# A planned kernel of linear attention and two MLPs: left rows of the attention's units as operations of their own, product half first, 10 warm-up transpositions for 24, look-ahead 22 for 20

## The chip, the cores and the metric

One core of one Trainium2 chip runs the whole program. The metric is the device time in microseconds; lower is better. The engines are TensorE (PE; its weight loads are shown as PEld), VectorE (DVE), ScalarE (ACT), GpSimd (POOL) and SyncE (SP), which issues nearly all of the DMA transfers here.

## The reference

Inputs and result are float32, except the weights of the MLPs, which are float64 and reach the kernel as pairs of 32-bit words. The attention is linear: for 4 batches and 8 heads, with 576 rows of width 64, it forms `kv = k^T v` per head, then `out = q kv`, and divides each row by its root mean square. Two MLPs follow on the 2304 x 512 result.

```
kv  = einsum('bhsd,bhse->bhde', k, v)
out = einsum('bhsd,bhde->bhse', q, kv)
out = out / sqrt(mean(out*out, -1) + 1e-6) * g_norm
x   = out as (2304, 512)
x   = softplus(x @ w_in)   @ w_out      # 512 -> 2048 -> 512
x   = max(0.01*h, h) @ w_out2,  h = x @ w_in2
```

## The kernel before

**Units.** The attention works in 16 units of one batch and two heads (`T`, `O`, `X`; unit u belongs to batch u // 4). Of the 576 rows of a unit, 512 are loaded as four blocks of 128 (`lda`, five buffers for each of q, k and v), and the other 64, the left rows, are loaded once per batch for all heads (`ldr`, two buffers). `T(u)` copies q and k into `qp` and `kp`, transposes q on PE in two halves (`f_t`: j = 0 writes the first PSUM bank of the unit, with two blocks and the left rows; j = 1 writes the second, with two blocks), multiplies k by v (`f_kv`, L436 and L439, in the second bank), masks the product into `kvm` (L455, L458) and copies the two banks to `qt` (L384, L386). The operations on one PSUM bank follow each other, so the second half of `qt` is copied only when `kvm` has been made. `O(u)` multiplies `qt` by `kvm` (`f_o`, L473; left rows `f_l`, L479) and takes squares and sums. `normal(w)` takes the units 2w and 2w + 1 together: logarithm and exponential on ACT, three Newton steps (L523 to L525) and the scaled outputs `xn` and `xnl` (L535) on DVE. Two PSUM banks hold the outputs, so `O(2w + 2)` waits for the `xn` of unit 2w. `X(u)` transposes `xn` back (L557, L569) and scales it into `xy` (L545, L547), which the MLPs read.

**Around it.** The weights are decoded from float64 on ACT and DVE (`decode_pair`, L609 to L649) and split into two parts (`split_pair`, L667 to L700). The first two pairs of chunks are decoded while the attention starts. The MLPs (lines 842, 932, 1099 and 1104 are their matmuls) run behind it, as far as possible already between the last units. Ahead of everything PE transposes the identity `N_WARM` times (`warm`, L1205).

**The order.** A planner, `Plan`, writes the order of every queue. Each operation is given its engines with a cost, what it reads and what it writes. Its due time is the sum of PE costs ahead of it in the program; an operation off PE is given `AHEAD` more (14 for the two first pairs of weights). Going backwards, the due time is then drawn forward to that of each reader less a latency of 0.2 and its own span (for a DMA 0.57 + 1.1 + its cost + 1.0). `run` simulates the engines with these costs, takes for each the operation with the earliest due time among those ready within 0.4 us, and emits it. An engine works through its queue strictly in the emitted order. A PE operation is one entry of the plan: all of its matmuls wait for all that it reads.

Of the kernel before, what the change touches and what calls it, by code (L numbers as in the profile page):

```python
# [21 lines left out]
class Plan:  # L22
# [2 lines left out]


    LAT = 0.2
    AHEAD = 20.0
    SPARE = 2.0
    WAIT = 0.4  # L30
    IDLE = 40.0
# [9 lines left out]
    def op(self, cost, fn, reads=(), writes=(), due=None):  # L41
        o = {"cost": cost, "fn": fn, "succ": [], "n": len(self.ops)}
        deps = {}
        for k in reads:
            if k in self.writer:
                deps[self.writer[k]["n"]] = self.writer[k]
        for k in writes:
            for d in [self.writer.get(k), *self.readers.get(k, ())]:
                if d is not None:
                    deps[d["n"]] = d  # L50
        for k in reads:
            self.readers.setdefault(k, []).append(o)
        for k in writes:
            self.writer[k], self.readers[k] = o, []
        o["deps"] = list(deps.values())
        for d in o["deps"]:
            d["succ"].append(o)
        o["due"] = self.pe
        if "PE" in cost:
            self.pe += cost["PE"]  # L60
        else:
            o["due"] += self.AHEAD
        if due is not None:
            o["due"] = due
        self.ops.append(o)
        return o
# [67 lines left out]
def linear_attention_two_mlps(  # L134
# [32 lines left out]
    nc = tc.nc  # L167
# [3 lines left out]
    P = 128  # L171
# [23 lines left out]
    GF = 4  # L195
    NG = NF // GF
    XL = 4
    N_WARM = 24
    U_H = 10


# [2 lines left out]
    def ring(pool, name, n, shape, dt=F32):  # L204
        return [pool.tile(shape, dt, name=f"{name}{i}") for i in range(n)]

    ident = const.tile([P, P], F32, name="ident")
# [112 lines left out]
    ps = ring(psum, "ps", 8, [P, 512])  # L320
# [6 lines left out]
    NLD = 5  # L327
    lda = {nm: ring(attp, nm + "a", NLD, [P, 2, 4, D]) for nm in "qkv"}
    ldr = {nm: ring(attp, nm + "r", 2, [P, H, D]) for nm in "qkv"}
    qp = ring(attp, "qp", 2, [P, 4, 2, D])  # L330
    kp = ring(attp, "kp", 2, [P, 4, 2, D])
# [5 lines left out]
    xnl = ring(mstp, "xnl", 2, [P, 4, D])  # L337
# [12 lines left out]
    op = plan.op  # L350
# [11 lines left out]
    def xyk(kcs, c0, n):  # L362
        return [("xy", kc, c) for kc in kcs for c in range(c0 // 64, (c0 + n - 1) // 64 + 1)]

    def copy_to(out, in_, n, reads, writes, engines="ADP"):


        def fn(e):
            if e == "A":
                nc.scalar.activation(out, in_, AF.Copy)  # L370
            elif e == "D":
                nc.vector.tensor_copy(out, in_)
            else:
                nc.gpsimd.tensor_scalar(out, in_, 1.0, 0.0, ALU.mult, ALU.add)

        cost = {"A": t_a(n), "D": t_d(n, True), "P": 0.1 + n * 1.2e-3}
        op({e: cost[e] for e in engines}, fn, reads, writes)

    def from_psum(out, in_, n, bank, writes):


        def fn(e):
            if e == "A":
                nc.scalar.activation(out, in_, AF.Copy)  # L384
            else:
                nc.vector.tensor_copy(out, in_)  # L386

        return op({"A": t_a(n), "D": t_d(n)}, fn, [], [("ps", bank), *writes])
# [22 lines left out]
    def T(u):  # L411
        b, hp = u // NPAIR, u % NPAIR
        h2 = slice(2 * hp, 2 * hp + 2)
        i = u % 2
        for nm, dst in (("q", qp), ("k", kp)):
            copy_to(
                dst[i], lda[nm][u % NLD].rearrange("p h r d -> p r h d"), 512,
                [(nm, u % NLD)], [(nm + "p", i)], "AD" if u == 0 else "ADP",
            )
        p0 = 2 * i if u < U_H else 0  # L420
        p1 = p0 + 1
        kv = ps[p1][:, 2 * P:3 * P]
        ql, kl, vl = (ldr[nm][b % 2] for nm in "qkv")
        va = lda["v"][u % NLD]

        def f_t(e, j):
            for r in range(2):
                nc.tensor.transpose(  # L428
                    ps[p0 + j][:, r * P:(r + 1) * P], qp[i][:, 2 * j + r, :, :], ident
                )  # L430
            if j == 0:
                nc.tensor.transpose(ps[p0][:, 2 * P:3 * P], ql[:, h2, :], ident)

        def f_kv(e):
            for r in range(4):
                nc.tensor.matmul(  # L436
                    kv, kp[i][:, r, :, :], va[:, :, r, :], start=(r == 0), stop=False
                )
            nc.tensor.matmul(kv, kl[:, h2, :], vl[:, h2, :], start=False, stop=True)  # L439

        for j in range(2):
            n = (2 * P + RL, 2 * P)[j]
            c0 = (0, 2 * P + RL)[j]
            op(
                {"PE": 0.25}, lambda e, j=j: f_t(e, j),
                [("qp", i)] + ([] if j else [("qr", b % 2)]), [("ps", p0 + j)],
            )
            if j:
                op(
                    {"PE": 1.1}, f_kv,  # L450
                    [("kp", i), ("v", u % NLD), ("kr", b % 2), ("vr", b % 2)], [("ps", p1)],
                )
                def f_m(e):
                    if e == "D":
                        nc.vector.tensor_tensor(kvm[i], kv, mask, ALU.mult)  # L455
                        return
                    for h in (slice(0, D), slice(D, P)):
                        nc.scalar.activation(  # L458
                            kvm[i][:, h], kv[:, h], AF.Copy, scale=mask[:, h.start:h.start + 1]
                        )  # L460

                op({"D": 0.22, "A": 0.42}, f_m, [], [("ps", p1), ("kvm", i)])
            from_psum(qt[i][:, c0:c0 + n], ps[p0 + j][:, :n], n, p0 + j, [("qt", i, j)])
# [3 lines left out]
    def O(u):  # L467
        i = u % 2
        at_ = (0, P, 2 * P + RL, 3 * P + RL)

        def f_o(e):
            for r in range(4):
                nc.tensor.matmul(  # L473
                    ps[4 + i][:, r * P:(r + 1) * P], qt[i][:, at_[r]:at_[r] + P], kvm[i],
                    start=True, stop=True,
                )

        def f_l(e):
            nc.tensor.matmul(  # L479
                ps[6][:, i * P:(i + 1) * P], qt[i][:, 2 * P:3 * P], kvm[i],  # L480
                start=True, stop=True,
            )

        need = [("kvm", i), ("qt", i, 0), ("qt", i, 1)]
        op({"PE": 0.87}, f_o, need, [("ps", 4 + i)])
        op({"PE": 0.22}, f_l, need, [("ps", 6)])
        squares(ps[4 + i], ("ps", 4 + i), sq[i], ss[u // 2 % 2][:, 8 * i:8 * i + 8], ("sq", i),
                ("ss", u // 2 % 2, i), P, 8)

    def squares(o, ok, s_, sum_, sk, mk, p, n):  # L490
        op(
            {"A": t_a(n * D)},
            lambda e: nc.scalar.activation(s_, o.rearrange("p (g d) -> p g d", d=D), AF.Square),
            [], [ok, sk],
        )
        op(
            {"D": t_d(n * D)},
            lambda e: nc.vector.tensor_reduce(sum_, s_, axis=AX, op=ALU.add), [sk], [mk],  # L498
        )
# [51 lines left out]
    def X(u):  # L551
        b, hp = u // NPAIR, u % NPAIR
        i = u % 2

        def f_x(e):
            for r in range(4):
                nc.tensor.transpose(  # L557
                    ps[7][:, r * P:(r + 1) * P], xn[u % 4][:, 2 * r:2 * r + 2, :], ident
                )

        cm, cl = (b * S + RL, b * S) if b % 2 else (b * S, b * S + 4 * P)
        op({"PE": 0.44}, f_x, [("xn", u % 4)], [("ps", 7)])
        scaled(xy[:, hp, cm:cm + 4 * P], ps[7], 4 * P, 7, xyk([hp], cm, 4 * P))
        if i == 0:
            return

        def f_l(e):
            for t in range(2):
                nc.tensor.transpose(  # L569
                    ps[6][:, (2 + t) * P:(3 + t) * P], xnl[u // 2 % 2][:, 2 * t:2 * t + 2, :], ident,  # L570
                )

        op({"PE": 0.11}, f_l, [("xnl", u // 2 % 2)], [("ps", 6)])
        scaled(
            xy[:, hp - 1:hp + 1, cl:cl + RL],
            ps[6][:, 2 * P:4 * P].rearrange("p (a n) -> p a n", a=2)[:, :, :RL],
            2 * RL, 6, xyk([hp - 1, hp], cl, RL),
        )
# [75 lines left out]
    def decode_pair(F, which, i):  # L654

        for m in range(2):
            decode_w(F + m, which, half[i][m])
# [545 lines left out]
    def warm(e):  # L1203
        for _ in range(N_WARM):
            nc.tensor.transpose(ps[7][:, 0:P], ident, ident)  # L1205

    op({"PE": 0.0}, warm, (), [("ps", 7)], due=-100.0)
    for i in range(NU + XL):
        if i in (1, 2):
            plan.AHEAD = 14.0  # L1210
            decode_pair(2 * (i - 1), 0, 0)
            split_pair(0, i - 1, True)
            plan.AHEAD = Plan.AHEAD
        if i < NU:
# [26 lines left out]
    for s in range(2 * NT2 + 2):  # L1241
        t, u = s // 2, s % 2
# [98 lines left out]
```

## Time and profile before

| | us |
|---|---|
| median of 3 runs (785.46 to 786.5) | 785.85 |
| the profiled execution | 782.83 |
| its span, first to last instruction | 780.9 |
| PE busy in it | 769.2 (98%) |
| DVE busy in it | 683.7 (88%) |
| ACT busy in it | 544.9 (70%) |

A row of the timeline gives the start, the length, the engine, the line and the operation with its tiles, the count, and in brackets the engine's idle time ahead of it and what ended it. In a list of waits each row gives the total, the number of waits and the longest one. A row of the windows gives, for each engine, busy time and instructions in a stretch; PEclk is TensorE's granted clock as a share of full speed.

### The profile page before, as it was taken

How to read it: one execution, taken by the hardware profiler on the slowest of the kernel's cores; microseconds unless marked ns; L12 is line 12 of the kernel's file. 1: busy time of each engine (PE TensorE's matmuls, PEld its weight loads, DVE VectorE, ACT ScalarE, POOL GpSimd, SP SyncE). 2: the span in 40 equal slices, each digit the busy share in tenths (PEclk: the TensorE clock that was granted, in tenths of full speed). 3: DMA queues.
4: the chain of work that ended last, by engine and by line, in shares of the span. 5: the costliest groups of instructions: out<-in, count | busy, mean ns of one | idle time of the engine just before them, and what ended most of it. 6: DMA issues, size and time to landing. Idle time of an engine off the chain costs nothing.

```text
span 780.9 us, 13269 instructions
## 1 busy us (share of the span) xinstructions
PE 769.2 (98%) x5053; PEld 765.3 (98%) x5053; DVE 683.7 (88%) x1088; ACT 544.9 (70%) x923; POOL 21.0 (3%) x36
## 2 busy tenths in 40 slices
PE   7899999999999999999999999999999999999997
PEld 7899999999999999999999999999999999999997
DVE  6999999999899987996899999998899877886667
ACT  5889989888687755774589788885668645554441
POOL 3330000000000000000000000000000000000000
PEclk9999999999999999999999999999999999999999
DMA  9992758675885783773678969785875762563814
GB/s 313 324 332 84 305 203 314 260 290 182 347 296 184 287 329 103 283 285 111 247 285 299 328 226 417 308 303 181 325 259 180 289 253 102 212 232 108 309 42 121
DMA packets 80351, 192.48 MB, mean 246 GB/s; under 512 B 11552, under 2 KB 54560, under 8 KB 80288
## 3 DMA queue, kind: packets, MB, share of 16 engines
q1 hardware_dynamic: 78672, 190.86, 67.5%
q10 hardware_dynamic: 1616, 0.79, 0.3%
q8 instruction: 39, 0.64, 0.3%
q14 instruction: 24, 0.20, 0.1%
HBM read 152.31 MB, written 39.32 MB: 245 GB/s over the span
## 4 chain that ended last, share of the span: by engine, by line
PE 94%; DVE 2%; ACT 1%; SPq 1%; DMA 1%; issue 0%; ACTq 0%; DVEq 0%
PE ps L842 43%; PE ps L1099 23%; PE ps L1104 22%; PE ps L473 2%; PE ps L932 2%; PE ps L436 1%; DMA mf<-in_moe_w_in_dram 1%; PE ps L557 1%; PE ps L428 0%; DVE ra L688 0%; DVE ss L498 0%; SPq L396 0%; DVE xn L535 0%; PE ps L479 0%; DVE mf L667 0%
## 5 line engine op out<-in xcount | busy, mean ns | idle before, releaser
L842 PE MATMUL ps<-ra 128*128 128x384 f32 x1932 | 385.5, 335 | 0.0
L842 PEld LDWEIGHTS ps<-ra 128*128 128x128 f32 x1932 | 332.1, 188 | 0.0
L1099 PE MATMUL ps<-rb 128*128 128x256 f32 x1512 | 203.9, 282 | 0.0
L1104 PE MATMUL ps<-rb 128*128 128x384 f32 x1008 | 200.9, 334 | 0.0
L1099 PEld LDWEIGHTS ps<-rb 128*128 128x128 f32 x1512 | 198.0, 189 | 0.1
L871 ACT ACTIVATE rb<-mf 128x768 fp32r<-128x768 f32 x154 | 130.0, 846 | 69.0 <-PE ps L1099 38.0
L1104 PEld LDWEIGHTS ps<-rb 128*128 128x128 f32 x1008 | 177.0, 188 | 0.0
L876 DVE TENSOR_TENSOR rb<-mf,rb 128x768 fp32r<-128x768 f32 x154 | 146.5, 953 | 23.7 <-ACT rb L871 22.8
L722 DVE TENSOR_TENSOR xy<-ps,xy 128x384 f32<-128x384 f32 (+2 forms) x247 | 134.6, 549 | 33.8 <-PE ps L1099 22.3
L956 DVE TENSOR_TENSOR mf<-mf 128x768 f32<-128x768 f32 x68 | 64.1, 951 | 2.7 <-ACT mf L857 2.1
L1149 ACT ACTIVATE mf<-ps 128x384 f32<-128x384 f32 x92 | 44.6, 488 | 28.5 <-PE ps L842 26.7
L1156 DVE TENSOR_TENSOR mf<-ps,mf 128x384 f32<-128x384 f32 x92 | 50.7, 553 | 11.1 <-PE ps L842 9.6
L1161 ACT ACTIVATE ps<-ps 128x384 f32<-128x384 f32 x46 | 22.0, 479 | 24.2 <-PE ps L842 24.1
L857 ACT ACTIVATE mf<-mf 128x768 f32<-128x768 f32 x26 | 21.9, 843 | 17.9 <-DVE mf L1156 17.6
L1021 DVE TENSOR_TENSOR rb<-rc,rb 128x512 fp32r<-128x512 f32 x44 | 29.9, 683 | 0.7 <-ACT rb L1018 0.7
L1018 ACT ACTIVATE rb<-rc 128x512 fp32r<-128x512 f32 x44 | 27.5, 625 | 1.4 <-PE ps L1099 0.8
L863 ACT ACTIVATE mf<-mf 128x768 f32<-128x768 f32 x24 | 20.1, 839 | 9.3 <-DVE mf L1156 9.3
L1115 ACT ACTIVATE ps<-ps 128x384 f32<-128x384 f32 (+2 forms) x44 | 21.0, 479 | 6.9 <-PE ps L1104 3.9
L635 ACT ACTIVATE sqr<-mf 128x512 uint16<-128x512 uint16 x30 | 23.4, 781 | 0.0
L863 ACT ACTIVATE mf<-ps 128x384 f32<-128x384 f32 x32 | 15.7, 490 | 9.8 <-PE ps L842 9.6
L717 ACT ACTIVATE xy<-ps 128x384 f32<-128x384 f32 (+2 forms) x38 | 18.6, 494 | 3.8 <-PE ps L1099 1.7
L857 ACT ACTIVATE mf<-ps 128x384 f32<-128x384 f32 x32 | 15.4, 482 | 6.6 <-PE ps L842 6.4
(123 smaller groups left out, 757.8 us busy)
## 6 DMA issues: line engine op xcount, KB each, us to landing
ra<-xscr SPq DMA_DIRECT2D x131, 768.0 KB, 6.6
xscr<-ra SPq DMA_DIRECT2D x30, 768.0 KB, 4.4
mf<-in_moe_w_in_dram SPq DMA_DIRECT2D x18, 512.0 KB, 5.2
mf<-in_moe_w_out_dram SPq DMA_DIRECT2D x18, 512.0 KB, 6.3
lf<-in_moe_w_in_dram SPq DMA_DIRECT2D x14, 512.0 KB, 5.4
lf<-in_moe_w_out_dram SPq DMA_DIRECT2D x14, 512.0 KB, 5.6
xscr<-xy SPq DMA_DIRECT2D x8, 768.0 KB, 5.5
qa<-in_q_dram SPq DMA_DIRECT2D x16, 256.0 KB, 5.3
```

The lines of the kernel that those rows point to most:

```text
L722: {"D": t_d(n)}, lambda e: nc.vector.tensor_tensor(dst, src, dst, ALU.add),
L842: nc.tensor.matmul(o, w_[:, a, c:c + P], e_[:, b, kk, :], start=(not on and which < 2 and kk == 0 and n == 0), stop=(kk == 1 and n == 2), ...
L857: {"A": t_a(n)}, lambda e: nc.scalar.activation(dst(), src(), AF.Softplus),
L863: lambda e: nc.scalar.activation(dst(), src(), AF.Prelu, alpha=0.01),
L871: {"A": t_a(n)}, lambda e: nc.scalar.activation(g[:, 0, :, :], c.ap, AF.Copy),
L876: lambda e: nc.vector.tensor_tensor(g[:, 1, :, :], c.ap, g[:, 0, :, :].bitcast(F32), ALU.subtract),
L956: lambda e: nc.vector.tensor_tensor(to.ap, x.ap, y.ap, ALU.subtract),
L1021: lambda e: nc.vector.tensor_tensor(w_[:, 1], src(), w_[:, 0].bitcast(F32), ALU.subtract), sk + hk, lk,
L1099: nc.tensor.matmul(y[:, 256 * (j % 2):256 * (j % 2 + 1)], G_[:, a, m, js], w_[:, b, m, :], **flags)
L1104: nc.tensor.matmul(y[:, :BN], w_[:, a, m, js], G_[:, b, m, :], **flags)
L1149: {"A": t_a(BN)}, lambda e: nc.scalar.activation(c[:, m, :], src, AF.Copy),
L1156: lambda e: nc.vector.tensor_tensor(c[:, m, :], src, c[:, m, :], ALU.add),
```

## The change

The planner's constant `AHEAD` goes from 20 to 22 and the warm-up from 24 to 10 transpositions. In `T` the transposition of the left rows (`f_tl`) and the product of the left rows (`f_kvl`) become operations of the plan of their own, so that only these read `ldr`. The half j = 1, which carries the product, is emitted ahead of the half j = 0. Some PE costs are changed, so that one 128-column pass counts 0.11.

```
-    AHEAD = 20.0
+    AHEAD = 22.0
-    N_WARM = 24
+    N_WARM = 10
 def T(u):
         def f_t(e, j):
             ...
-            if j == 0:
-                nc.tensor.transpose(ps[p0][:, 2 * P:3 * P], ql[:, h2, :], ident)
+
+        def f_tl(e):
+            nc.tensor.transpose(ps[p0][:, 2 * P:3 * P], ql[:, h2, :], ident)
 
         def f_kv(e):
             for r in range(4):
                 nc.tensor.matmul(
                     kv, kp[i][:, r, :, :], va[:, :, r, :], start=(r == 0), stop=False
                 )
+
+        def f_kvl(e):
             nc.tensor.matmul(kv, kl[:, h2, :], vl[:, h2, :], start=False, stop=True)
 
-        for j in range(2):
+        for j in (1, 0):
             ...
             op(
-                {"PE": 0.25}, lambda e, j=j: f_t(e, j),
-                [("qp", i)] + ([] if j else [("qr", b % 2)]), [("ps", p0 + j)],
-            )
+                {"PE": 0.22}, lambda e, j=j: f_t(e, j),
+                [("qp", i)], [("ps", p0 + j)],
+            )
+            if j == 0:
+                op({"PE": 0.11}, f_tl, [("qr", b % 2)], [("ps", p0)])
             if j:
-                op(
-                    {"PE": 1.1}, f_kv,
-                    [("kp", i), ("v", u % NLD), ("kr", b % 2), ("vr", b % 2)], [("ps", p1)],
-                )
+                op({"PE": 0.89}, f_kv, [("kp", i), ("v", u % NLD)], [("ps", p1)])
+                op({"PE": 0.22}, f_kvl, [("kr", b % 2), ("vr", b % 2)], [("ps", p1)])
 def O(u):
-        op({"PE": 0.87}, f_o, need, [("ps", 4 + i)])
+        op({"PE": 0.89}, f_o, need, [("ps", 4 + i)])
 def X(u):
-        op({"PE": 0.11}, f_l, [("xnl", u // 2 % 2)], [("ps", 6)])
+        op({"PE": 0.22}, f_l, [("xnl", u // 2 % 2)], [("ps", 6)])
```

## Rows read from the trace of the kernel before

**Rows 1.** The page, part 1: busy us, share of the span, instructions, by engine.
```profile
PE 769.2 (98%) x5053; PEld 765.3 (98%) x5053; DVE 683.7 (88%) x1088; ACT 544.9 (70%) x923; POOL 21.0 (3%) x36
```

**Rows 2.** Waits of PE over the span: us in total, times, longest us.
```profile
PE ps L473 <- DVE xn L535: 1.5, 1, 1.5
PE ps L432 <- DMA qr<-in_q_dram: 0.9, 1, 0.9
PE ps L557 <- ACT xy L545: 0.6, 1, 0.6
PE ps L473 <- DVE kvm L455: 0.6, 1, 0.6
PE ps L557 <- DVE xy L547: 0.6, 1, 0.6
PE ps L932 <- ACT mf L384: 0.4, 1, 0.4
PE ps L428 <- ACT qp L370: 0.4, 1, 0.4
PE ps L569 <- DVE xnl L535: 0.4, 1, 0.4
```

**Rows 3.** Timeline of PE, 0 to 30 us.
```profile
1.96 5.04 PE L1205 MATMUL ps<-ident 128*128 128x128 f32 x24 [1.96 <-POOL ident masks.py:199]
6.83 0.60 PE L428 MATMUL ps<-ident,qp 128*128 128x128 f32 x4
...
10.54 1.16 PE L473 MATMUL ps<-kvm,qt 128*128 128x128 f32 x8 [0.59 <-DVE kvm L455]
11.91 1.16 PE L436 MATMUL ps<-va,kp 128*128 128x128 f32 x8 [0.22 <-DMA va<-in_v_dram]
...
15.25 1.06 PE L473 MATMUL ps<-kvm,qt 128*128 128x128 f32 x8
...
21.36 1.16 PE L473 MATMUL ps<-kvm,qt 128*128 128x128 f32 x8 [1.51 <-DVE xn L535]
```

**Rows 4.** Windows: length, busy us of PE, PEld, DVE, ACT, POOL, PEclk, DMA.
```profile
15.00:20.00 5.00, 3.96 (x34) 3.53 (x33) 4.90 (x10) 4.55 (x12) 2.40 (x3) 1.00 1.14 361
...
100.00:140.00 40.00, 40.00 (x233) 40.00 (x232) 38.99 (x57) 34.73 (x58) 0.00 (x0) 1.00 0.68 260
```

**Rows 5.** Timeline of all engines, 16 to 22 us: DVE ahead of PE's wait.
```profile
18.44 1.22 DVE L688 TENSOR_TENSOR ra<-mf,ra 128x1024 fp32r<-128x1024 f32 x1
...
20.62 0.69 DVE L535 TENSOR_TENSOR xn<-ps,fm 128x512 f32<-128x512 f32 x1
```

**Rows 6.** Timeline of all engines, 0 to 16 us: DVE behind loads.
```profile
3.45 0.71 DVE L372 COPY qp<-qa 128x512 f32<-128x512 f32 x1 [1.94 <-DMA qa<-in_q_dram]
...
11.15 0.47 DVE L629 TENSOR_SCALAR sqr<-mf 128x512 uint16<-128x512 uint16 x1 [0.34 <-DMA mf<-in_moe_w_in_dram]
```

**Rows 7.** The same timeline: loads issued by SP.
```profile
0.75 0.44 SPq L396 DMA_DIRECT2D qa<-in_q_dram  x1
...
1.25 0.45 SPq L595 DMA_DIRECT2D mf<-in_moe_w_in_dram  x1
...
1.75 0.51 SPq L396 DMA_DIRECT2D ka<-in_k_dram  x1
...
2.30 0.74 SPq L405 DMA_DIRECT2D qr<-in_q_dram  x1
...
3.08 0.61 SPq L396 DMA_DIRECT2D qa<-in_q_dram  x1
...
3.74 0.47 SPq L396 DMA_DIRECT2D va<-in_v_dram  x1
...
6.26 0.47 SPq L595 DMA_DIRECT2D mf<-in_moe_w_in_dram  x1
```

**Rows 8.** Durations of transpositions, ns: least, median, most; first and last start.
```profile
L1205 PE MATMUL ps<-ident x24: 273/418/473, 2.0 to 6.7; 128*128 128x128 f32 x24
L428 PE MATMUL ps<-ident,qp x64: 272/273/328, 6.8 to 64.6; 128*128 128x128 f32 x64
```

## The prediction

> **What bounds the kernel now.** I read the page's busy row first: TensorE (PE) is busy 769.2 of 780.9 us, so at most 11.7 us can be had without taking work from it [rows 1]. The list of PE's waits comes next, because it says where those 11.7 us lie [rows 2]. With the 1.96 us before its first instruction and the 0.22 us for v of unit 1, both to be seen in the timeline [rows 3], the ten waits of the list come to 7.6 us. The other 4.1 us, by subtraction, lie behind PE's last matmul. The longest waits stand in the first 30 us, and in a stretch of the MLPs such as 100 to 140 us PE is busy 40.00 of 40.00 us [rows 4]. So all that the change can win lies in the attention, and about 5.6 us of it are waits.
>
> In the attention's first 20 us the timeline [rows 3] shows PE with its warm-up until the first transposition at 6.83, the first output product at 10.54, and the second (unit 1) at 15.25; at 21.36 PE waits 1.51 us for DVE. DVE is the busy engine there: 4.90 of 5.00 us from 15 to 20 us [rows 4]. Its rows just before that wait are a weight split of 1.22 us that stands ahead of the first normalisation, which ends in xn at 20.62 [rows 5]. So the chain to follow is: output of unit 1, squares, sums, normalisation on DVE, and only then the output of unit 2, since both use one PSUM bank. How early unit 1's output runs, and what DVE has in hand, sets the gain; the warm-up itself is not a step of that chain.
>
> **Fewer warm-up transpositions.** The 24 take 5.04 us [rows 3], 0.21 us each from start to start. Taking 14 away saves 2.9 us of PE time and PE is free at 1.96 + 10 x 0.21 = 4.1. The copy of q for unit 0 starts at 3.45 and takes 0.71 [rows 6], to 4.16. So the first transposition can start at 4.2 and not at 6.83: 2.6 us earlier, of which nothing is won yet, because the product needs k and v.
>
> **Costs, order and left rows: the loads.** The planner orders what it emits by due times, so I worked the dues of the first loads out by hand; they give an order here, and no time. A load's due is that of its reader less 3.6 (0.2 + 0.57 + 1.1 + 0.73 + 1.0), and less 0.69 more where a copy lies between. Before: q0 -4.29, k0 -3.79, left q -3.60, q1 -3.36 (unit 1 is drawn forward by the bank of unit 2's output), v0, left k and left v -3.10, k1 -2.91, v1 -2.22. The rows of issue show this order, with the first weight chunk between q0 and k0 and the second at 6.26, behind k1 [rows 7]. With the product half first, its left rows apart and the costs of the diff: q0 -4.69, k0 -4.27, v0 -3.58, q1 -3.28, k1 -2.86, left k and v -2.49, v1 -2.17, left q -2.05. The weight chunks move by at most 0.14 (the position of PE at which they are emitted), so the first falls behind k0, and the second stays near left k and v.
>
> Landings are by bytes. From the landing of q0 at 3.45 to that of v1, on which PE waits until 11.91 [rows 3, 6], ten transfers of together 2.75 MB (256 KB for q, k or v of a unit, 512 for a chunk, 128 for left rows, from the shapes) land in 8.46 us, 325 GB/s, or 0.81 us for 256 KB. In the new order: k0 at 4.3, first chunk 5.9, v0 6.7, q1 7.5, k1 8.3, left k and v 9.1, second chunk 10.7 (11.15 before, [rows 6]; between 9.9 and 11.5 by its place), v1 11.5, left q 11.9. So **the product of unit 0** can run at 6.7 and not behind 8.4. But its output needs the left rows of q, at 11.9, then a transposition and a copy of 0.49 us: it goes from 10.54 to about 12.8. I cost this at nothing, because nothing waits for the output of unit 0 alone: the normalisation takes units 0 and 1 together. If that cover is gone it costs up to one output, 1.1 us [rows 3] (the third rival).
>
> **Output of unit 1.** Its product can start with v1 at 11.5, 0.4 earlier, and runs 1.1 us; kvm and the copy of qt take 0.7 us, so it could run at 13.5 to 14.0 behind the output of unit 0, if the planner puts it ahead of unit 2's product; otherwise it stays at 15.25. That is 0 to 1.5 us. On DVE the second chunk's work starts 0.45 us earlier (0 to 1.2 by its place), and DVE has no idle time to give later. I take 0.8 us for the normalisation, between DVE's 0.45 and PE's 1.25, since both have to come earlier. The bounds are 0 and 1.5.
>
> **The new waits.** The separate left-row operations stand in PE's one queue. Behind the left transposition stand the outputs; behind the left product stands what makes kvm, for which DVE waits. Unit 4, whose left rows belong to the next batch, shows the price: 0.9 us on left q [rows 2]. But PE then waited for DVE's xn anyway, so I cost taking this wait away at nothing: what is late next is xn. It can cost from -0.9 to +0.9 us; I take 0, by the wait that follows it.
>
> **Longer look-ahead and the small costs.** AHEAD 22 moves the due of weight and x work that no near reader holds by 2 us behind copies that PE waits for. The waits that this could end are the ones on ACT xy (0.6), ACT mf (0.4) and DVE xnl (0.4) [rows 2], 1.4 us at best. The other end is as large: the same work done too late stops PE as long, and 0 of slack on DVE near 20 us speaks for that. I take 0.3 us of gain, nearer to nothing, since ACT and DVE are only put in another order. In the MLPs PE waits for nothing now, so there is no gain there and no row that prices a loss.
>
> **The clock.** A warm-up transposition takes 418 ns in the median, at least 273; those of the attention take 272 to 328 [rows 8]. Their spacing is 0.21 us in the warm-up (5.04 over 24) and 0.11 in unit 0 (0.60 for four, of which the last counts 0.27, [rows 3]), so the first ones ran at the lower of the two levels (1.2 GHz) and the last at 2.4, after PE had been busy without a break since 1.96. The clock column shows 1.00 in all stretches and doesn't tell this; I go by the durations. With 10, PE has a gap from about 5.0 to 6.7 and may be at 1.2 GHz in unit 0. There 15 passes (10 of the product, 5 transpositions) take 0.10 more each, 1.5 us, and they lie between 6.7 and 11.5, where PE waits for v1: hidden. Only a lower clock beyond 11.5 costs.
> The Trainium skill's "TensorE: Matmul & The Clock Gate" says in Part 1 that the clock starts low, that activity releases it and that idle time gives it back, which speaks against this cut; the rows agree on the start and the rise, and none of PE's gaps here, 1.5 us at most, let it fall. Its Part 4 says that transpositions do not engage the full clock; these rows disagree, since nothing but transpositions ran when 418 became 273. By Part 4 the 14 would be worth nothing and the last rival below would fall away.
>
> **The sum.** The profiled execution took 782.83 us, 1.93 around its span of 780.9. 782.83 - 0.8 (normalisation) - 0.3 (look-ahead) = 781.7. The median of the runs is 785.85, 3.0 above the profiled execution; on it the same 1.1 us give 784.7.
>
> **Rivals.**
> *More comes free:* unit 1's output moves the full 1.5, and the waits on xy, mf and xnl go with it (1.4): 785.85 - 2.9 = 782.9. For it speaks that PE has the work in hand as soon as DVE lets it; against it, that DVE is full.
> *DVE holds:* the split stays ahead of the normalisation, xn comes at 20.62 as before, PE only waits longer: 785.85. The full DVE speaks for it, the second chunk that lands earlier against it.
> *Left rows too late:* the output of unit 0 at 12.8 pushes that of unit 1 behind it and behind unit 2's product: +1.1 us, 786.9. It decides if unit 1's output starts later than 15.25.
> *The clock stays low,* and the kernel is slower: if PE is at 1.2 GHz beyond 11.5 up to unit 1's output, that is 10 passes of product, 10 of output 0, 2 left transpositions and 10 of output 1, 32 x 0.10 = 3.2 us late, less the 1.1 of the forecast: 785.85 + 2.1 = 788.0. For it speaks that the clock rose in the trace only behind work without a break; against it, that PE has work at 1.2 GHz from 6.7 to about 10 with hardly a break.
>
> **How the numbers follow.** Forecast 784.7, own range 783.3 to 785.9: 0.42. More comes free 0.15, DVE holds 0.17, left rows late 0.10, clock 0.16. A measurement of this kernel tells about 0.2%, 1.6 us, from no change. Faster by that: the 0.15 and 0.17 of the forecast's 0.42, 0.32. Slower: 0.16 of the clock and 0.02 of the left rows' case, 0.18. Same: 0.50. The range goes from 782.7, just below the case of more gain, to 787.5, which leaves most of the clock's case out and some of the tail below.
>
> **What would show it.** Right: first transposition at about 4.2; issue order q0, k0, chunk, v0, q1, k1; unit 1's output (second group of L473's kind) at 14.0 to 14.5; xn at about 19.8; PE without waits from 100 us on. DVE holds: unit 1's output earlier, xn still at 20.6. Clock: passes spaced 0.21 beyond 11.5 us. Wrong altogether: waits of PE in the MLPs, or left q loaded early as before.

## The result and the profile after

The changed kernel took 789.98 us (median of 5 runs, 789.12 to 792.05) beside 785.56 for the kernel before: a ratio of 1.006, 95% interval 1.0041 to 1.0079, so 4.7 us (3.2 to 6.2) slower. Forecast were 784.7 us and a range that ended at 787.5. The profiled execution took 789.12 us with a span of 787.2, 6.3 us more than in the profiled execution of before. That one (782.83) was 2.4 us faster than the fastest of the 5 runs of before here, so differences between the two traces overstate the change.

The busy row of the page of after, to be held against [rows 1]:

```profile
PE 772.1 (98%) x5039; PEld 767.5 (98%) x5039; DVE 684.0 (87%) x1089; ACT 543.7 (69%) x926; POOL 19.2 (2%) x35
```

PE's waits over the span in after, to be held against [rows 2]:

```profile
PE ps L442 <- DMA vr<-in_v_dram: 2.3, 1, 2.3
PE ps L437 <- DMA va<-in_v_dram: 2.2, 2, 2.0
PE ps L560 <- DVE xy L550: 2.0, 1, 2.0
PE ps L1208 <- POOL ident masks.py:199: 2.0, 1, 2.0
PE ps L845 <- DMA ra<-xscr: 1.0, 1, 1.0
PE ps L560 <- ACT xy L548: 0.8, 1, 0.8
```

PE executes 14 instructions fewer and is busy 2.9 us longer, so some of its work ran slower. The longest waits are now on loads (left v, and v), and one is new in kind: L845, a matmul of the MLPs, waits 1.0 us for x from DRAM (`xscr`). In the kernel before PE had no wait behind 85 us.

The timeline of PE, 0 to 40 us, answers [rows 3]:

```profile
1.96 2.40 PE L1208 MATMUL ps<-ident 128*128 128x128 f32 x10 [1.96 <-POOL ident masks.py:199]
4.21 1.03 PE L428 MATMUL ps<-ident,qp 128*128 128x128 f32 x4
7.20 1.13 PE L437 MATMUL ps<-va,kp 128*128 128x128 f32 x8 [1.96 <-DMA va<-in_v_dram]
...
11.87 0.77 PE L442 MATMUL ps<-vr,kr 128*128 128x128 f32 x2 [2.28 <-DMA vr<-in_v_dram]
12.91 2.04 PE L437 MATMUL ps<-va,kp 128*128 128x128 f32 x8 [0.28 <-DMA va<-in_v_dram]
...
15.70 3.46 PE L476 MATMUL ps<-kvm,qt 128*128 128x128 f32 x16
...
24.32 1.16 PE L476 MATMUL ps<-kvm,qt 128*128 128x128 f32 x8
```

The first transposition starts at 4.21. But the left product waits until 11.87, the outputs of units 0 and 1 run behind each other from 15.70 (10.54 and 15.25 before), and 16 passes take 3.46 us, 0.21 each: the lower level of the clock. The output of unit 2 comes at 24.32, 2.96 us later than before. The windows of after show the clock (the column ahead of the last two):

```profile
5.00:10.00 5.00, 2.48 (x14) 1.68 (x12) 2.24 (x5) 1.62 (x3) 0.40 (x2) 0.84 1.09 341
10.00:15.00 5.00, 2.85 (x12) 2.62 (x13) 3.07 (x6) 1.52 (x2) 1.08 (x2) 0.50 1.13 317
15.00:20.00 5.00, 5.00 (x30) 4.71 (x30) 3.84 (x8) 3.18 (x6) 0.97 (x2) 0.63 1.09 384
...
30.00:35.00 5.00, 3.78 (x23) 3.78 (x24) 4.47 (x14) 3.28 (x10) 1.56 (x2) 0.73 1.14 288
```

The clock did rise (the eight passes at 7.20 take 1.13 us, as at the upper level), and fell again between 5 and 10 us, after PE had stood 1.96 us in front of v; it fell a second time between 30 and 35, after the 1.97 us in front of DVE's xy.

The loads, issued by SP, answer [rows 7]:

```profile
1.25 0.45 SPq L396 DMA_DIRECT2D ka<-in_k_dram  x1
...
1.74 0.47 SPq L598 DMA_DIRECT2D mf<-in_moe_w_in_dram  x1
...
2.25 0.51 SPq L396 DMA_DIRECT2D va<-in_v_dram  x1
...
3.83 0.47 SPq L598 DMA_DIRECT2D mf<-in_moe_w_in_dram  x1
...
4.34 0.76 SPq L405 DMA_DIRECT2D kr<-in_k_dram  x1
...
6.15 1.32 SPq L396 DMA_DIRECT2D va<-in_v_dram  x1
...
7.52 0.61 SPq L405 DMA_DIRECT2D qr<-in_q_dram  x1
```

That is the order worked out from the due times; the second weight chunk took the place ahead of left k and v, the earliest of those that the forecast left open.

Now the two places of the loss. The rows of one line give its least, median and longest duration and the start of its first and last instruction. PE's first matmul of the MLPs on `ra` (L842, after the change L845) and its last on `rb` (L1099, L1102) bound the MLPs, before:

```profile
L842 PE MATMUL ps<-ra x1932: 334/334/339, 86.2 to 759.7; 128*128 128x384 f32 x194
L1099 PE MATMUL ps<-rb x1512: 278/282/385, 437.8 to 776.5; 128*128 128x256 f32 x189
```

and after:

```profile
L845 PE MATMUL ps<-ra x1932: 334/334/444, 90.3 to 765.9; 128*128 128x384 f32 x194
L1102 PE MATMUL ps<-rb x1512: 277/282/388, 440.9 to 782.7; 128*128 128x256 f32 x189
```

The MLPs start 4.1 us later, and then take 692.4 us (90.3 to 782.7) and not 690.3: 2.1 us are lost in a stretch where the forecast expected nothing to happen. This pair of rows is the measure used below, "the MLPs' stretch". In the six kernels with a look-ahead of 20 in the MLPs and no wait of PE there it lay between 690.2 and 690.6. The start of the MLPs is a poor measure: two kernels with the same attention start them up to 3.1 us apart (run 5).

### The profile page after: what moved, and what is told of

Same layout as the page of the kernel before. It is cut to its first block, busy times and chain, and to the rows that moved or that the text cites. A ratio compares the mean times of both kernels' runs of the same rounds, so it can differ in the third digit from the quotient of the medians.

```text
span 787.2 us, 13265 instructions
## 1 busy us (share of the span) xinstructions
PE 772.1 (98%) x5039; PEld 767.5 (98%) x5039; DVE 684.0 (87%) x1089; ACT 543.7 (69%) x926; POOL 19.2 (2%) x35
## 4 chain that ended last, share of the span: by engine, by line
PE 94%; DMA 2%; DVE 1%; ACT 1%; SPq 1%; issue 0%; ACTq 0%; DVEq 0%
PE ps L845 42%; PE ps L1102 22%; PE ps L1107 22%; PE ps L476 2%; PE ps L437 2%; PE ps L935 2%; DMA ra<-xscr 1%; DMA va<-in_v_dram 1%; PE ps L560 1%; PE ps L428 1%; PE ps L482 0%; PE ps L442 0%; SPq L396 0%; DVE ss L501 0%; SPq L405 0%
## 5 line engine op out<-in xcount | busy, mean ns | idle before, releaser
L845 PE MATMUL ps<-ra 128*128 128x384 f32 x1932 | 386.2, 335 | 1.1 <-DMA ra<-xscr 1.0
L845 PEld LDWEIGHTS ps<-ra 128*128 128x128 f32 x1932 | 332.1, 188 | 1.7 <-ACT mf L1152 1.2
L1102 PE MATMUL ps<-rb 128*128 128x256 f32 x1512 | 204.2, 282 | 0.0
L1102 PEld LDWEIGHTS ps<-rb 128*128 128x128 f32 x1512 | 198.1, 189 | 0.3 <-ACT xy L720 0.2
L1152 ACT ACTIVATE mf<-ps 128x384 f32<-128x384 f32 x92 | 44.9, 489 | 28.6 <-PE ps L845 27.5
L866 ACT ACTIVATE mf<-ps 128x384 f32<-128x384 f32 x32 | 15.7, 490 | 9.8 <-PE ps L845 9.3
L691 DVE TENSOR_TENSOR ra<-mf,ra 128x768 fp32r<-128x768 f32 (+1 forms) x18 | 19.5, 1084 | 1.9 <-ACT ra L687 1.9
```

Source lines behind the costliest of these rows:

```text
L845: nc.tensor.matmul(o, w_[:, a, c:c + P], e_[:, b, kk, :], start=(not on and which < 2 and kk == 0 and n == 0), stop=(kk == 1 and n == 2), ...
L866: lambda e: nc.scalar.activation(dst(), src(), AF.Prelu, alpha=0.01),
L1102: nc.tensor.matmul(y[:, 256 * (j % 2):256 * (j % 2 + 1)], G_[:, a, m, js], w_[:, b, m, :], **flags)
L1152: {"A": t_a(BN)}, lambda e: nc.scalar.activation(c[:, m, :], src, AF.Copy),
```

## The experiments

Theories at the start: **load order** (left rows come last, outputs 0 and 1 are late), **clock** (too few warm-up transpositions), **look-ahead** (the planner's 22). Ratios are against runs of the kernel before on the same chip.

**1. The warm-up alone.** In the kernel before:
```
-    N_WARM = 24
+    N_WARM = 10
```


> The kernel before with 10 warm-up transpositions and nothing else; the order of every queue stays. Clock theory: PE stops between the warm-up and the first products (k0 lands only at 6.2, q1 at 7.2), the granted clock falls or rises late, the outputs of units 0 and 1 (10.5 and 15.25 before) run at 1.2 GHz for some passes: 1 to 3 us slower than before. Load-order theory: the loads come as before, so no more than 0.3 us of change either way; the first transposition moves to about 4.2.

Measured: 786.78 us, ratio 1.0025 (1.0008 to 1.0043), 2.0 us. The MLPs' stretch is 690.3 (88.5 to 778.8). In the timeline of PE:

```profile
9.44 1.98 PE L436 MATMUL ps<-va,kp 128*128 128x128 f32 x8
...
22.84 1.16 PE L473 MATMUL ps<-kvm,qt 128*128 128x128 f32 x8 [2.17 <-DVE xn L535]
```

The product of unit 0 takes 1.98 us and not 1.06 as at the upper level, and the output of unit 2 comes 1.48 us later than in [rows 3]. So the clock theory holds for the order of before: 14 transpositions less cost about 2.0 us (0.6 to 3.4).

**2. The warm-up back, in the changed kernel.**
```
-    N_WARM = 10
+    N_WARM = 24
```


> The changed kernel with 24 warm-up transpositions; the order of every queue is that of the changed kernel. Clock theory: the clock is at 2.4 GHz when the outputs of units 0 and 1 run, these take 1.7 us less together (16 passes of 0.21 become 0.11): 1.5 to 3 us faster than the changed kernel, about 787. Load-order theory: PE still waits for the left rows of v until about 11.9 and for v1 until 12.9, so less than 1 us is won, about 789.5, and the clock may fall in that gap all the same.

Measured: 790.66 us, 1.0072 (1.005 to 1.0094): nothing won that can be told. The MLPs' stretch is 693.9 us, 1.5 longer than in after with the same order of the other engines' queues, so the whole time alone doesn't price the warm-up here. PE stood 2.4 us in front of the product of unit 0 and 2.3 us in front of left v, and the clock fell all the same (0.66 between 15 and 20 us). In the new order the clock fell behind these waits, whatever the warm-up; run 7 fills them.

**3. Look-ahead back to 20, in the changed kernel.**
```
-    AHEAD = 22.0
+    AHEAD = 20.0
```


> The changed kernel with a look-ahead of 20. If the longer look-ahead has a part in the loss, the wait of PE for x at the start of the second MLP (1.0 us) goes, and 1 us or more is won: about 788.5 to 789. If the loss lies in the first 35 us alone, the time stays within 0.5 us of the changed kernel's 790.

Measured: 791.5 us, 1.0083 (1.0064 to 1.0101). Neither half of the expectation held: nothing was won, and the time isn't within 0.5 us of 790. The wait for x is gone and the MLPs' stretch is 691.1 us (94.8 to 785.9), 1.3 us less than after. But between 77 and 95 us PE now waits 2.6 us for ACT's copies (L935 on L384) and runs at the lower clock behind that, so the MLPs start at 94.8. In them PE waits 0.54 us for ACT at 453.86. A single constant undone in a planner's order isn't that part of the change undone.

**4. Left rows of the first batch early,** in the changed kernel:
```
+                first = {"q": -4.0, "k": -3.4, "v": -3.4}[nm] if b == 0 else None
-                op({"S": 0.73}, fn, (), [(nm + "r", b % 2)])
+                op({"S": 0.73}, fn, (), [(nm + "r", b % 2)], due=first)
```


> The changed kernel with the left rows of the first batch given due times by hand, so that left q is issued fourth and left k and v right behind v0, as before the change. Load-order theory: the left product no longer waits (2.28 us) for left v, the outputs of units 0 and 1 start some 2 to 3 us earlier than at 15.7, and 2 to 4 us are won: 786 to 788. Clock theory: the gap of PE between 5.2 and 7.2 stays, the clock still falls at about 8, and less than 1.5 us is won.

Measured: 792.03 us, 1.0087 (1.0066 to 1.0109). PE's timeline shows that it does what it was made for:

```profile
12.05 1.45 PE L477 MATMUL ps<-kvm,qt 128*128 128x128 f32 x8 [0.48 <-DVE kvm L459]
...
16.27 1.16 PE L477 MATMUL ps<-kvm,qt 128*128 128x128 f32 x8
```

The outputs come at 12.05 and 16.27, and the one of unit 2 still at 24.07, 0.25 us earlier than after. The MLPs' stretch is 697.5 us (89.3 to 786.8), with one wait of 3.4 us for x. Behind it the granted clock is 0.62 (445 to 450 us) and 0.70 (450 to 455), and the next twelve passes on `ra` take 4.18 us where those behind the wait in after take 2.32: a wait there can cost more than its own length. The MLPs lost 5.1 us more than in after, so the whole time doesn't price the attention. But late outputs of units 0 and 1 alone don't set unit 2. DVE works from 14.72 to its xn at 23.33 with one break of 0.2 us, and 4.6 us of that, behind the output of unit 1, are weight splits (L671, L692); PE waits 1.2 us more for v at 22.07. The load-order theory, which looked for 2 to 4 us from early outputs, falls in this form.

**5. Look-ahead 22 alone,** in the kernel before:
```
-    AHEAD = 20.0
+    AHEAD = 22.0
```


> The kernel before with a look-ahead of 22 and nothing else. PE's order is that of before up to the MLPs, so the attention and the first matmuls of the first MLP (86.2) stay where they were. If the longer look-ahead is what makes PE wait for x at the start of the second MLP (about 440 us), the first matmuls of the second MLP and the end come 1 to 3 us later than before; if that wait comes from the attention's new order, less than 0.5 us.

Measured: 789.86 us, 1.0043 (1.0028 to 1.0059), 3.4 us: most of the whole change, from the one constant. Its rows of the two lines:

```profile
L842 PE MATMUL ps<-ra x1932: 334/334/446, 89.3 to 767.1; 128*128 128x384 f32 x194
L1099 PE MATMUL ps<-rb x1512: 277/282/387, 439.8 to 784.0; 128*128 128x256 f32 x189
```

The MLPs' stretch is 694.7 us, 4.4 more than before. The order of every queue up to 86 us is that of before, and yet the MLPs start 3.1 us later than in the profiled execution of before: left q of unit 4 came 1.8 us late and not 0.9, v1 1.3 and not 0.2. Behind the wait for left q the granted clock is 0.72 (20 to 25 us), and the outputs of units 2 and 3 take 1.93 and 1.75 us, not 1.16 and 1.06. That much lies in the landing of loads and the clock behind it, from one execution to the next, so starts of the MLPs in single traces don't tell the attention of two kernels apart.

Where the 4.4 us are lost, SP's rows tell. Before:

```profile
422.85 0.39 SPq L595 DMA_DIRECT2D lf<-in_moe_w_in_dram  x1
425.26 0.34 SPq L825 DMA_DIRECT2D ra<-xscr  x1
427.61 4.65 SPq L806 DMA_DIRECT2D xscr<-xy  x2
433.91 0.34 SPq L825 DMA_DIRECT2D ra<-xscr  x1
...
435.95 0.32 SPq L825 DMA_DIRECT2D ra<-xscr  x1
```

With 22, SP's rows:

```profile
429.28 0.33 SPq L825 DMA_DIRECT2D ra<-xscr  x1
429.71 0.38 SPq L595 DMA_DIRECT2D lf<-in_moe_w_in_dram  x1
430.15 5.15 SPq L806 DMA_DIRECT2D xscr<-xy  x2
439.02 0.33 SPq L825 DMA_DIRECT2D ra<-xscr  x1
...
440.98 0.43 SPq L825 DMA_DIRECT2D ra<-xscr  x1
```

and PE's waits in its timeline from 436 to 500 us:

```profile
445.10 2.32 PE L842 MATMUL ps<-ra 128*128 128x384 f32 x12 [1.65 <-DMA ra<-xscr]
...
458.07 1.31 PE L842 MATMUL ps<-ra 128*128 128x384 f32 x6 [1.48 <-DMA ra<-xscr]
```

The 3.1 us of the later start taken off, the weight chunk (`lf`) is issued 3.8 us later than before, now directly ahead of the two stores of x, and the two loads of x 2.0 us later. In SP's waits from 415 to 452 us the loads of x (L825) stand behind the stores of x. Before:

```profile
SPq L825 <- DMA xscr<-xy: 5.0, 4, 1.9
```

With 22:

```profile
SPq L825 <- DMA xscr<-xy: 16.1, 4, 6.4
```

PE then waits 1.65 and 1.48 us for the loads. In the trace of before the load issued at 433.91 landed at 439.87, and the matmul that waits for it stands at 439.97: there was 0.1 us to spare, where the same load now comes 2.0 us later. The changed kernel shows the same pattern (`lf` at 430.84, stores at 431.28, loads at 439.66 and 441.61) and a wait of 0.99 us at 445.29.

**6. Early left rows and 24 transpositions,** the edits of 2 and 4 together:
```
-    N_WARM = 10
+    N_WARM = 24
+                first = {"q": -4.0, "k": -3.4, "v": -3.4}[nm] if b == 0 else None
```

> The changed kernel with the left rows of the first batch loaded early and 24 warm-up transpositions. If late left rows and the low clock are the two causes of the 4.15 us in the attention, and either alone leaves the other in place, the first matmul L845 of the first MLP comes within 1 us of 86.2 (89.3 with early left rows alone). If the causes lie in the order of PE's later units, it stays beyond 88.5. The wait for x near 440 us is likely to stay, so the whole time says less: 787 to 790.

Measured: 790.91 us, 1.0061 (1.0045 to 1.0077). The MLPs start at 91.3 and take 693.3 us, with a wait of 2.2 us for x. The first bound (within 1 us of 86.2) is missed, and by its letter 91.3, beyond 88.5, speaks for the order of PE's later units. But by what run 5 shows of such starts both bounds were too sharp; inconclusive for the attention.

**7. Fillers in the gaps,** in the changed kernel (`fill` transposes the identity into a bank that is not yet in use):
```
         def f_kv(e):
+            if u == 0:
+                fill(10)
...
         def f_kvl(e):
+            if u == 0:
+                fill(16)
```


> The changed kernel in its own order of queues, with 10 transpositions of the identity ahead of the product of unit 0 and 16 ahead of its left product, in the gaps where PE waits for loads. They keep PE busy from 1.96 to about 12. Clock theory: outputs of units 0 and 1 run at 2.4 GHz, 16 passes in 1.8 and not 3.46 us, and the MLPs start 1.5 to 3 us earlier than at 90.3: 787 to 788.5. If the clock has no part, 90.3 and 790 stay.

Measured: 790.48 us, 1.0064 (1.0048 to 1.008). The clock stays at the upper level from 5.1 us on (ten fillers at 5.13 take 1.29 us), and the 16 passes of outputs 0 and 1 take 2.05 us and not 3.46. The MLPs start at 89.4, 0.9 us earlier than after and within the spread of run 5; their stretch is 694.3 us. The output of unit 2 comes at 23.80, 0.5 us earlier. So the low clock, plain as it is in the trace of after, isn't the main cause of the loss in the changed kernel: the intervals of the two ratios leave at most 1.6 us for it.

**8. Left rows apart and new costs, the rest as before:** halves (0, 1), 24 transpositions, look-ahead 20, in the changed kernel.
```
-    AHEAD = 22.0
+    AHEAD = 20.0
-    N_WARM = 10
+    N_WARM = 24
-        for j in (1, 0):
+        for j in (0, 1):
```


> The changed kernel with the old order of halves (0, 1), 24 warm-up transpositions and a look-ahead of 20, which is the kernel before with the left rows apart and the new PE costs. Left q is issued fourth again, left k and v go behind v1. If the order of halves (left q last, outputs of units 0 and 1 late) carries the attention's loss, the first MLP's first matmul is within 1 us of 86.2; if the separate left rows and the costs carry it, it is at 88 or later.

Measured: 786.31 us, 1.0013 (1.0001 to 1.0025), 1.0 us. The MLPs' stretch is 690.3 us (88.8 to 779.1). By the expectation's letter, 88.8 speaks for left rows and costs; by run 5 it says nothing, and the ratio is what counts.

**9. Look-ahead 22 in the attention, 20 in the MLPs,** in the changed kernel:
```
+    plan.AHEAD = 20.0
     for s in range(2 * NT2 + 2):
```


> The changed kernel with its look-ahead of 22 in the attention and 20 from the MLPs' loop on. Look-ahead theory (the loss is made at the start of the second MLP, where weight loads come late and push the stores and loads of x): PE's waits for x from DRAM near 440 us go, the stretch from the first matmul of the first MLP to PE's last one is that of the kernel before (690.3 us from 86.2 to 776.5), and the time falls by 2 to 4.5 us to 785.5 to 788. Attention theory (the loss is made by left rows, order of halves and clock): 788.5 or more.

Measured: 787.94 us, 1.0023 (1.0011 to 1.0035). The rows of the two lines:

```profile
L845 PE MATMUL ps<-ra x1932: 334/334/339, 92.5 to 766.0; 128*128 128x384 f32 x194
L1102 PE MATMUL ps<-rb x1512: 278/282/388, 444.1 to 782.8; 128*128 128x256 f32 x189
```

The MLPs' stretch is 690.3 us again, to the tenth that of before, and PE waits for nothing behind 93 us. So the longer look-ahead in the MLPs costs 1.006 less 1.0023, about 2.9 us (1.1 to 4.7, from the two intervals) of the change's 4.7; the other 1.8 us (0.9 to 2.8) belong to the attention.

**10. Look-ahead 20 for the weights alone,** in the changed kernel:
```
         F = (g + 1) * GF
+        plan.AHEAD = 20.0
         ...
+        plan.AHEAD = Plan.AHEAD
```


> The changed kernel with a look-ahead of 20 for the decoding and splitting of weights in the MLPs alone; x and all else keep 22. If the weights' loads are what comes late, this gives as much as 20 for the whole of the MLPs: 785.5 to 788, without waits for x near 440 us. If the later parts of x themselves are what comes late, the wait stays and the time is 789 or more.

Measured: 789.19 us, 1.0047 (1.0031 to 1.0064); the MLPs' stretch is 693.0 us (88.6 to 781.6). `lf` goes back to 425.29, the stores to 430.04, the loads to 436.62 and 438.57, all within 0.3 us of before when the start's 2.4 us are taken off, and the wait at 445 us is gone. But PE now waits 0.40 us for ACT at 442.27, 0.31 at 449.84 and 0.67 for x at 454.68. The pattern of run 5 is where the time was lost there, and mending it alone didn't bring it back.

**11. Both: look-ahead 20 in the MLPs and 24 transpositions,** in the changed kernel:
```
-    N_WARM = 10
+    N_WARM = 24
+    plan.AHEAD = 20.0
     for s in range(2 * NT2 + 2):
```

> The changed kernel with a look-ahead of 20 in the MLPs and 24 warm-up transpositions. Beside the same kernel with 10 it prices the warm-up without the wait near 440 us: clock theory, 0.5 to 2 us faster than with 10; by the run of the changed kernel with 24 (790.66 beside 789.98) nothing.

Measured: 787.74 us, 1.0014 (1.0 to 1.0028), MLPs' stretch 690.6 us. Beside run 9 that is 0.7 us for the warm-up, with intervals that overlap: not told from nothing.

**12. Fillers in the kernel before,** 8 ahead of unit 4's left transposition, 12 and 3 ahead of the outputs of units 2 and 4, into columns that are not in use.
```
             if j == 0:
+                if u == 4:
+                    fill(8)
...
         def f_o(e):
+            if u in (2, 4):
+                for _ in range(12 if u == 2 else 3):
+                    nc.tensor.transpose(ps[2 * (u // 2 % 2)][:, 3 * P:], ident, ident)
```


> The kernel before with transpositions of the identity where PE waits in the attention: 8 ahead of the left rows of unit 4, 12 ahead of the output of unit 2, 3 ahead of that of unit 4. If the clock's falls in PE's gaps make the spread of the runs of before (782.8 to 788.7), the spread narrows and the median falls by 0.5 to 1.5 us; if the loads make it, median and spread stay.

Measured: 785.57 us (783.73 to 787.22), 0.9998 (0.9986 to 1.0011). The same as before. Its 11 runs spread over 3.5 us and the 29 of before beside it over 5.3, but with standard deviations of 1.1 and 1.3 us that isn't narrower by anything that can be told. By the expectation, that speaks for the loads as what spreads the runs, not for the clock; neither is shown. No kernel here beats the kernel before.

**13. Look-ahead 22 for the weights and 20 for all else in the MLPs,** in the changed kernel, the counterpart of 10:
```
+    plan.AHEAD = 20.0
     for s in range(2 * NT2 + 2):
         ...
         F = (g + 1) * GF
+        plan.AHEAD = 22.0
         ...
+        plan.AHEAD = 20.0
```

> The changed kernel with a look-ahead of 22 for the decoding and splitting of weights in the MLPs and 20 for all else there, the counterpart of the run with 20 for the weights alone (789.19, MLPs 693.0 us from their first matmul to PE's last). Weights theory: the weights alone make the wait, so the waits for x near 440 us stay and the MLPs take 692.4 us or more. Theory of x: the later parts of x make it, and the MLPs take 690.3 to 691 us, as with 20 for everything. If both fall short, only the two together restore the order, and the loss belongs to no single kind of work.

Measured: 790.77 us, 1.008 (1.0065 to 1.0095); the MLPs' stretch is 693.7 us (90.6 to 784.3), with 0.71 us for ACT at 441.94 and 1.10 for x at 446.96. By the letter of the expectation this speaks for the weights, but run 10, with the weights at 20, lost 2.7 us as well: 22 for either kind of work is enough for a loss.

**14. Look-ahead 18,** in the kernel before:
```
-    AHEAD = 20.0
+    AHEAD = 18.0
```


> The kernel before with a look-ahead of 18. If a longer look-ahead harms because work for the second MLP comes too late, a shorter one leaves the MLPs at 690.3 us or less of PE time and the whole within 1 us of before. If each value only deals the order anew, the MLPs may take 691 to 695 us at 18 too, with a wait in another place.

Measured: 789.59 us, 1.007 (1.0048 to 1.0091); the MLPs' stretch is 694.5 us (90.4 to 784.9), with 1.26 and 0.42 us for x at 450.23 and 457.62 and 0.66 us for ACT at 507.23. A shorter look-ahead loses in the same place as the longer one, and a little further on.

Taken together, the MLPs' stretch by the look-ahead in the MLPs:

| look-ahead there | kernels | stretch, us |
|---|---|---|
| 20 | before, 1, 8, 9, 11, 12 | 690.3, 690.3, 690.3, 690.3, 690.6, 690.2 |
| 20, with ACT's wait at 88 us | 3 | 691.1 |
| 22 | after, 2, 4, 5, 6, 7 | 692.4, 693.9, 697.5, 694.7, 693.3, 694.3 |
| mixed | 10, 13 | 693.0, 693.7 |
| 18 | 14 | 694.5 |

Where PE waits, the stretch doesn't repeat: after, 2 and 7 have one order of the other engines' queues and differ by 1.9 us, 4 and 6 another one and differ by 4.2. So a single trace tells a loss from 690.3, but not one of these orders from the next.

## Why the prediction was wrong

**The step that failed** is the look-ahead's. The forecast took 0.3 us of gain for it, looked for its effect in the attention's waits, and closed the MLPs with "there is no gain there and no row that prices a loss". The loss was made there: by the constant alone the kernel lost 3.4 us (run 5), and setting it back in the MLPs alone takes away 2.9 of the whole change's 4.7 (run 9 beside after). PE's 40.00 us of 40.00 [rows 4] were read as a stretch that a new order can't touch. They say only that the order of before had no wait. How little lay between that order and a wait stood in the trace near 430 us, which the forecast never read: two stores of x that hold SP for 4.65 us, loads of x that stand behind them, and one of these landing 0.1 us ahead of its matmul. What the forecast called a mark of being wrong altogether, waits of PE in the MLPs, came true, and no rival stood for it; so the range ended 2.5 us too early.

**The loads** were right in order, one by one, and mis-sized in time: landings were put at 7.5 for q1, 10.7 for the second chunk, 9.1 for left v and 11.5 for v1. The engines that wait for them went on at 7.79, 10.83, 11.87 and 12.91. Left v fell behind the second chunk, the end of the range that was named, and SP needed 0.97 to 1.32 us for an issue there, two to three times the 0.44 to 0.51 of its first ones.

**The output of unit 1** was forecast at 13.5 to 14.0, or 15.25; both outputs went from 15.70 on. This is the rival of the late left rows in its worst form, and the xn it was to bring forward came at 23.58 and not 19.8. But run 4 made the outputs early and won 0.25 us at unit 2: the chain from unit 1's output to unit 2's, on which the 0.8 us rested, has more in it than that output. In run 4 it was DVE with its weight splits, which is the mechanism of the rival that DVE holds; its xn came at 23.33, later than the 20.62 that the rival put.

**The clock rival** named its mark, passes of 0.21 us beyond 11.5 us, and the trace shows it. The price of 3.2 us doesn't hold: run 1 gives 2.0 us (0.6 to 3.4) for the cut in the order of before, and in the changed order neither the warm-up (runs 2 and 11) nor fillers (run 7) bring a gain that can be told; a part of up to 1.6 us stays possible (run 7). The reason given against it, that PE has work with hardly a break, fell with the loads: PE stood 1.96 us in front of v and 2.28 in front of left v.

**The attention as a whole** costs 1.8 us (0.9 to 2.8, run 9), where 1.1 us of gain were forecast, 0.3 of them by the look-ahead. Left rows apart with the new costs give 1.0 us of it (0.1 to 2.0, run 8), and with the order of halves turned and 22 in the attention as well 1.1 (0 to 2.2, run 11), so these two together add nothing that can be told. The warm-up's share is between nothing and the 2.0 us of run 1.

**What stays open:** which single operation of the MLPs has to keep its place. Weights alone at 20 and all else alone at 20 both lose (runs 10 and 13), and so does 18 for all (run 14). What is shown is that the other orders lost 0.8 to 7.2 us in the MLPs, and that all of PE's waits over 0.2 us there stood between 440 and 460 us, at the start of the second MLP, but for 0.66 us (run 14) and 0.33 us (run 13) near 507. Which of the attention's parts makes its 1.8 us is open as well.

## What to carry to other kernels

A planner's constant is an edit of the whole program. Its price must be looked for wherever the schedule has no slack, and a stretch without waits is not one with slack: read how late the last thing lands that it needs. Compare such variants by a stretch of the trace that repeats from run to run (here the MLPs' 690.3 us, which repeats only as long as PE doesn't wait in it) and not by the place where a change was meant to act, and undo a part by the region it works in (run 9), since undoing the constant everywhere deals a new order (run 3).

## What the runs showed of the hardware

PE's clock fell after PE had stood 1.96 us between two short groups of work (after: granted clock 0.84 from 5 to 10 us, 0.50 from 10 to 15), but not after 3.18 us in front of v in run 8 (1.00 from 10 to 20 us), so the length of a gap alone doesn't tell. It was up from 5.1 us on in run 7, behind transpositions alone; with 24 of them it fell as well once PE had stood 2.4 us in front of a product and 2.3 us in front of left v (run 2: 0.66 from 15 to 20 us). Ahead of its first rise the column of the granted clock reads 1.00 while passes run at the lower level: in run 1 the product at 9.44 takes 1.98 us for eight passes, and the column shows 1.00 from 5 to 15 us, so there the durations have to be read. And the same attention, in the same order, reached the MLPs at 86.2 and at 89.3 us in two executions: loads landed later in the second, and behind the longest wait for one, 1.8 us, the clock fell to 0.72 (20 to 25 us).
